# Large loads in two halves of 64 partitions, one issued by SyncE and one by ScalarE: a decode block on one core of a Trainium2 chip

## The chip, the cores and the metric

The kernel runs on one core of one Trainium2 chip. A core has TensorE (PE in the profile; its weight loads, PEld, are listed apart), VectorE (DVE), ScalarE (ACT), GpSimd (POOL), SyncE (SP), which here only issues transfers, and 16 DMA engines that move data between the chip's memory (HBM) and the on-chip memory of 128 partitions (SBUF). Each engine works through its own instructions in order; a DMA is issued by an instruction in the queue of one of the engines. The metric is the time of one execution in microseconds on the device. Most executions of one kernel agree within 0.3%.

## The reference

One decode step of a transformer block with adaptive layer norm, four sequences, one new token each, all in float32. Cut to what matters:

```python
B, Sq, D = 4, 1, 512;  H, Sk, Dh = 32, 4096, 128;  F = 1792
mod = silu(c) @ w_mod                          # six vectors of 512: sa, ca, ga, sb, cb, gb
h = layernorm(x) * (1 + ca) + sa
q = (h @ wq) as (B, H, 1, Dh)
scores = einsum("bhqd,bhkd->bhqk", q, k_cache) * Dh ** -0.5
o = einsum("bhqk,bhkd->bhqd", softmax(scores), v_cache)
x = x + ga * (o @ wo)
h = layernorm(x) * (1 + cb) + sb
out = x + gb * (silu(h @ w1) @ w2)
```

The two caches are 4 x 32 x 4096 x 128 float32 each, 268 MB apiece. Every byte of them is read once and used for one multiplication and one addition.

## The kernel before

**Tiles.** A cache tile holds four heads of one sequence: 4 heads x 4096 positions are spread over 128 partitions, 128 positions to a partition, so that a partition receives one contiguous run of 128 x 128 float32 (64 KB) and a tile has 8 MB. There are N = 32 such tiles of K and 32 of V, n = 0 to 31, with b = n % 4 the sequence and t = n // 4 the group of heads.

**Three slots.** All large data live in three slots of 64 KB per partition (`Slot`, pool `kv`, `bufs=3`), which are taken in turn: w_mod, wq, k0, v0, k1, v1, ... So k(n+1) takes the slot of v(n-1), and v(n+1) that of k(n). A load is issued when the last reader of what its slot held has finished. The first slot, that of w_mod, also holds the small tensors of the opening (`cg`, `csT`, `qs`, `zsel`), and v0 takes it.

**Order.** The body stands under `manual_schedule()`: each engine issues its instructions in the order in which the program emits them. Before the change all large loads go through `fetch` (L84) or stand at L126 and L129, on SP's queue. ACT issues four small loads of `c` at the start (L123), four of `x` in iteration 28, and two of the four output writes.

**Opening.** `c` lands, silu and a transpose make `csT` (L174, L175, L178); `mods` multiplies it with w_mod (L190, L202); after the layer norm come q = h @ wq (L237), its spreading over partitions (L247, L252) and the first four rows of q (`make_qb(0)`: four Copies on ACT at L260, a matmul at L262, one Copy at L266). Then v0 can be loaded.

**Iteration n** emits, in this order: `load_k(n+1)`; the product K x q in place, 40 of the 128 positions on POOL and 88 on DVE (`mult`, L271); `make_qb(n+1)` (ACT L266; where n+1 is a multiple of four also ACT L260 and PE L262 ahead of it); `vsum(n-1)`, two matmuls on PE at L324 that are the last readers of v(n-1); the sums over Dh on DVE (`red`, L276); the row maximum and its spreading (`rowmax` L280, `bmax` L284 on PE, `negmax` L289 to L292); the exponential on ACT and its layout on POOL (`softexp`, L298, L302); `load_v(n+1)`; the first 32 positions of V multiplied and added on POOL (`vmult`, L314, L318); and the other 96 on PE (`pv`, L339).

**End.** The last K tile is loaded in two cuts along the free dimension; wo is loaded in iteration 31 in four cuts into the slot of the last V but one, w1 and w2 in nine cuts behind the last softmax, all by `fetch`. Then follow the projection, the second layer norm and the feed-forward part.

Of the kernel before, what the change touches and what calls it, by code (L numbers as in the profile page):

```python
# [17 lines left out]
def kernel(  # L18
# [13 lines left out]
    nc = tc.nc  # L32
    P = 128
# [8 lines left out]
    NJ = HP * S // P  # L42
# [13 lines left out]
    N = B * NT  # L56
# [11 lines left out]
    class Slot:  # L68
# [4 lines left out]
        def take(self, *shape):  # L73
# [5 lines left out]
            names = " ".join(f"a{i}" for i in range(len(shape)))  # L79
            return v.rearrange(f"p ({names}) -> p {names}", **{f"a{i}": s for i, s in enumerate(shape)})  # L80

    def fetch(t, src, *cuts):
        for lo, hi in zip(cuts, cuts[1:]):
            nc.sync.dma_start(t[:, lo:hi], src[:, lo:hi])  # L84
# [3 lines left out]
    def load(dst, cache, name, n, *cuts):  # L88
        t, b = divmod(n, B)
        dst[n] = Slot(f"{name}{n}").take(NJ, Dh)  # L90
        src = cache[b, HP * t : HP * (t + 1)].rearrange("h (p j) d -> (h p) j d", p=QW)
        fetch(dst[n], src, *(cuts or (0, NJ)))

    def load_k(n, *cuts):
        load(kt, kc, "k", n, *cuts)

    def load_v(n):
        load(vt, vc, "v", n)

    wmv = wm.rearrange("(p k) n -> p k n", p=P)  # L100
    wqv = wq.rearrange("(p k) n -> p k n", p=P)
# [5 lines left out]
    wmt = s0.take(NK, 6 * D)  # L107
# [15 lines left out]
        nc.scalar.dma_start(cg[W * g : W * g + B, :], c[:, g * P : (g + 1) * P])  # L123
    for g in range(G):
        nc.gpsimd.dma_start(x0[W * g : W * g + B, :], xr[:, g * P : (g + 1) * P])
    nc.sync.dma_start(wmt, wmv)  # L126
    s1 = Slot("wq")
    wqt = s1.take(NK, H * Dh)
    nc.sync.dma_start(wqt, wqv)  # L129
    load_k(0)  # L130

    ident = const.tile([P, P], F32, name="ident")
# [123 lines left out]
    def make_qb(n):  # L256
        if n % B == 0:
            m = work.tile([P, B, Dh], F32, tag="o", name=f"qm{n}", bufs=1)
            for b in range(B):
                nc.scalar.activation(m[:, b, :], qn, AF.Copy, scale=sel[:, n + b : n + b + 1])  # L260
            p = psum([P, B, Dh], "q", 2)
            nc.tensor.matmul(p, blk.rearrange("p i x -> p (i x)"), m, start=True, stop=True)  # L262
            for b in range(B):
                qb[n + b] = p[:, b, :]
        qw[n] = work.tile([P, Dh], F32, tag="qw", name=f"qw{n}")
        nc.scalar.activation(qw[n], qb[n], AF.Copy)  # L266
# [3 lines left out]
    def mult(eng, src, n, lo, hi):  # L270
        eng.tensor_mul(  # L271
            kt[n][:, lo:hi, :], kt[n][:, lo:hi, :], src[n].unsqueeze(1).to_broadcast([P, hi - lo, Dh])
        )

    def red(n, lo, hi):
        nc.vector.tensor_reduce(sc[n][:, lo:hi], kt[n][:, lo:hi, :], axis=AX.X, op=ALU.add)  # L276

    def rowmax(n):
        nm[n] = work.tile([P, 1], F32, tag="rm", name=f"rm{n}")
        nc.vector.tensor_reduce(nm[n], sc[n], axis=AX.X, op=ALU.max)  # L280

    def bmax(n):
        p = psum([P, P], "mx", 2)
        nc.tensor.transpose(p, nm[n].to_broadcast([P, P]), ident)  # L284
        nm[n] = p

    def negmax(n):
        m = work.tile([P, HP], F32, tag="hx", name=f"hx{n}")
        nc.vector.tensor_reduce(m, nm[n].rearrange("p (i x) -> p i x", i=HP), axis=AX.X, op=ALU.max)  # L289
        nc.vector.tensor_mul(m, m, hn)  # L290
        nm[n] = work.tile([P, 1], F32, tag="nm", name=f"nm{n}")
        nc.vector.tensor_reduce(nm[n], m, axis=AX.X, op=ALU.add)  # L292

    def softexp(n):
        t, b = divmod(n, B)
        if b == 0:
            rs[t] = work.tile([P, B], F32, tag="rs", name=f"rs{t}")
        nc.scalar.activation(sc[n], sc[n], AF.Exp, bias=nm[n], accum_out=rs[t][:, b : b + 1])  # L298
        for h in range(2):
            f = first(n) if h == 0 else 0  # L300
            m = HG - f
            nc.gpsimd.tensor_mul(  # L302
                pz[h][:, f * W : HG * W].rearrange("p (g x) -> p g x", g=m)[:, :, E:].rearrange("p g (i j) -> p g i j", i=HP),
                sc[n][:, JJ * (HG * h + f) : HG * JJ * (h + 1)].rearrange("p (g j) -> p g j", j=JJ)
                .unsqueeze(2).to_broadcast([P, m, HP, JJ]),
                hm.unsqueeze(1).unsqueeze(3).to_broadcast([P, m, HP, JJ]),
            )

    def first(n):
        return NV // JJ if n < N - 2 else 0  # L310

    def vmult(n):
        if first(n):
            nc.gpsimd.tensor_mul(  # L314
                vt[n][:, :NV, :], vt[n][:, :NV, :], sc[n][:, :NV].unsqueeze(2).to_broadcast([P, NV, Dh])
            )
            for m in (NV // 2, NV // 4, JJ):
                nc.gpsimd.tensor_add(vt[n][:, :m, :], vt[n][:, :m, :], vt[n][:, m : 2 * m, :])  # L318

    def vsum(n):  # L320
        t, b = divmod(n, B)
        q, a = divmod(b, 2)
        o = (1 - a) * E
        nc.tensor.matmul(  # L324
            po[t, q][0:W, :], hs[:, o : o + W], vt[n][:, :JJ, :].rearrange("p j d -> p (j d)"),
            start=False, stop=a == 1,
        )
# [20 lines left out]
    def gather(t, q):  # L348
        o = work.tile([P, JJ, Dh], F32, tag="o", name="o", bufs=1)
        nc.vector.tensor_mul(  # L350
            o, po[t, q].rearrange("p (j d) -> p j d", j=JJ), jm.unsqueeze(2).to_broadcast([P, JJ, Dh])
        )
        if q == 0:
            od[t] = psum([P, Dh], "od", 1)
        s = work.tile([P, Dh], F32, tag="lnu", name="s", bufs=1)
        nc.vector.tensor_reduce(s, o.rearrange("p j d -> p d j"), axis=AX.X, op=ALU.add)  # L356
        nc.tensor.matmul(od[t], spick[:, 2 - 2 * q : 2 - 2 * q + P], s, start=q == 0, stop=q == 1)  # L357
# [3 lines left out]
    def norm(t):  # L361
        p = psum([P, B], "mx", 2)
        nc.tensor.matmul(p, blk.rearrange("p i x -> p (i x)"), rs[t], start=True, stop=True)
        m = work.tile([P, B], F32, tag="dx", name="dx")
        nc.vector.tensor_mul(m, p, xm)
        rd[t] = work.tile([P, 2], F32, tag="rd", name="rd")
        nc.vector.tensor_reduce(rd[t][:, 0:1], m, axis=AX.X, op=ALU.add)
        nc.vector.reciprocal(rd[t][:, 1:2], rd[t][:, 0:1])

    def spread(t):  # L370
        on = work.tile([P, R, QW], F32, tag="lnu", name="on", bufs=1)
        nc.vector.tensor_scalar(
            on, od[t].rearrange("p (x r) -> p r x", r=R), rd[t][:, 1:2], None, op0=ALU.mult
        )
        ot = work.tile([P, R, W], F32, tag="ot", name="ot", bufs=1)
        nc.vector.transpose(ot, on)
        nc.vector.tensor_copy(oz[:, t], ot[:, :, :B])
# [14 lines left out]
    for n in range(N):  # L392
        t, b = divmod(n, B)
        if n < N - 2:
            load_k(n + 1)
        elif n == N - 2:
            load_k(n + 1, 0, NJ // 2, NJ)
        else:
            so = Slot("wo")
            wot = so.take(NT, R, D)  # L400
            fetch(wot, wov, 0, NT // 2, NT - 2, NT - 1, NT)
        if n == N - B:
            for g in range(G):
                nc.scalar.dma_start(xg[W * g : W * g + B, :], xr[:, g * P : (g + 1) * P])
        sc[n] = work.tile([P, NJ], F32, tag="sc", name=f"sc{n}")
        if n + 1 < N:
            mult(nc.gpsimd, qw, n, 0, NA)
            mult(nc.vector, qb, n, NA, NJ)
            make_qb(n + 1)
            if n and first(n - 1):  # L410
                vsum(n - 1)
            red(n, NA, NJ)
        else:
            for lo in (0, NJ // 2):
                mid, hi = lo + NL // 2, lo + NJ // 2
                mult(nc.gpsimd, qw, n, lo, mid)
                mult(nc.vector, qb, n, mid, hi)
                red(n, mid, hi)
        if n and b == 0:
            gather(t - 1, 1)  # L420
        if b == 2:
            gather(t, 0)
        if n + 1 < N:
            red(n, 0, NA)
        else:
            for lo in (0, NJ // 2):
                red(n, lo, lo + NL // 2)
        if n and b == 0:
            spread(t - 1)
        rowmax(n)  # L430
        bmax(n)
        negmax(n)
        softexp(n)
        if n + 1 < N:
            load_v(n + 1)
        else:
            s2 = Slot("w12")
            w1t = s2.take(NK, F)
            w2t = s2.take(NI, D)
            fetch(w1t, w1v, 0, 2, 3, 4)  # L440
            fetch(w2t, w2v, 0, 4, 8, 11, 12, 13, 14)
        if b == B - 1:
            norm(t)
        vmult(n)
        pv(n)
# [74 lines left out]
```

## Time and profile before

| what | value |
|---|---|
| time, median of 3 runs | 1323.12 us (1322.90 to 1323.14) |
| the profiled execution's own time | 1323.02 us |
| its span, first to last instruction | 1321.1 us |
| moved by DMA | 567.66 MB, 430 GB/s over the span |
| busy: DVE | 1011.0 us (77%) |
| busy: POOL | 844.9 us (64%) |
| busy: PE | 381.0 us (29%) |
| busy: ACT | 45.2 us (3%) |

The share of an engine is the time in which it worked on instructions, over the span; registers, branches, waits and the issuing of DMAs are not counted. A DMA queue has a row of its own: q1 carries what SP issues, q10 what ACT issues, q0 what POOL issues; q8 and q14 load instructions. Its packets, bytes and the share of the 16 DMA engines' time that they took stand beside it. In a timeline line stand the start, the duration, the engine, the line of the program and the operation; in brackets the idle time before it and what ended that.

### The profile page before, as it was taken

The numbers are of one execution on the slowest core, as the hardware profiler recorded it, in microseconds if no ns is written. First come the engines' busy times: TensorE is split into PE (matmuls) and PEld (weight loads), VectorE is DVE, ScalarE is ACT, GpSimd is POOL, SyncE is SP. The second block draws the span as 40 slices with busy tenths as digits, with TensorE's granted clock in tenths as the row PEclk, the third lists the DMA queues.
The fourth block names the chain that finished last, engine by engine and source line by source line (L and its number), as shares of the span: only waits on it lengthen the run. The fifth ranks groups of instructions, "written<-read, shape, count | busy, mean of one in ns | idle before, by whom it ended". The sixth has DMA issues, their size and how long they took to land.

```text
span 1321.1 us, 5438 instructions
## 1 busy us (share of the span) xinstructions
PE 381.0 (29%) x2114; PEld 98.8 (7%) x2114; DVE 1011.0 (77%) x362; ACT 45.2 (3%) x148; POOL 844.9 (64%) x231
## 2 busy tenths in 40 slices
PE   3421133222222233222322322233321223322047
PEld 0100000000000000000000000000000000000013
DVE  2378877877888777898778788787779877787982
ACT  1100000000000000000000000000000000000001
POOL 1236787575678756577865756877565786657550
PEclk9855666665566666566666556666655666655569
DMA  9999999999999999999999999999999999999998
GB/s 413 443 415 442 439 421 437 437 427 437 433 431 435 435 431 433 433 435 433 433 427 437 435 429 435 439 429 429 439 429 433 441 429 429 434 437 429 425 425 341
DMA packets 12282, 567.66 MB, mean 430 GB/s; under 512 B 1441, under 2 KB 1505, under 8 KB 2273
## 3 DMA queue, kind: packets, MB, share of 16 engines
q1 hardware_dynamic: 12048, 567.29, 99.5%
q8 instruction: 17, 0.28, 0.1%
q14 instruction: 9, 0.07, 0.0%
q0 software_dynamic: 128, 0.01, 0.0%
q10 hardware_dynamic: 80, 0.02, 0.0%
HBM read 567.30 MB, written 0.01 MB: 429 GB/s over the span
## 4 chain that ended last, share of the span: by engine, by line
DVE 39%; DMA 32%; POOL 19%; another core or an unknown queue 4%; PE 3%; issue 2%; ACT 1%; DVEq 0%; POOLq 0%; ACTq 0%
DMA k<-in_A_k_cache_dram 29%; DVE sc L276 21%; DVE k L271 14%; POOL v L318 9%; POOL v L314 8%; DMA w<-in_B_w_dram 3%; PE po L324 2%; DVE s L356 1%; POOL pz L302 1%; POOL k L271 1%; DVE o L350 1%; ACT sc L298 1%; PE mx L284 1%; DVE hx L289 0%
## 5 line engine op out<-in xcount | busy, mean ns | idle before, releaser
L276 DVE TENSOR_REDUCE sc<-k 128x88 f32<-128x11264 f32 (+2 forms) x66 | 554.4, 8422 | 1.1
L271 DVE TENSOR_TENSOR k<-k,q 128x11264 f32<-128x11264 f32 (+1 forms) x33 | 378.4, 11467 | 217.9 <-DMA k<-in_A_k_cache_dram 217.9
L271 POOL TENSOR_TENSOR k<-k,qw 128x5120 f32<-128x5120 f32 (+1 forms) x33 | 356.2, 10796 | 53.1 <-DMA k<-in_A_k_cache_dram 53.1
L302 POOL TENSOR_TENSOR pz<-sc,hm 128x128 f32<-128x128 f32 (+1 forms) x64 | 31.5, 512 | 378.7 <-ACT sc L298 378.7
L339 PE MATMUL po<-v,pz 128*32 128x512 f32 x1568 | 239.5, 775 | 44.3 <-POOL pz L302 44.2
L318 POOL TENSOR_TENSOR v<-v 128x2048 f32<-128x2048 f32 (+2 forms) x90 | 244.6, 2717 | 7.1
L314 POOL TENSOR_TENSOR v<-v,sc 128x4096 f32<-128x4096 f32 x30 | 211.0, 7033 | 0.0
L324 PE MATMUL po<-v,hs 128*32 128x512 f32 x60 | 57.4, 1061 | 249.4 <-POOL v L318 249.4
L284 PE MATMUL mx<-ident,rm 128*128 128x128 f32 x32 | 14.5, 454 | 385.9 <-DVE rm L280 385.9
L357 PE MATMUL od<-s,spick 128*128 128x128 f32 x32 | 12.2, 484 | 217.5 <-DVE s L356 217.5
L339 PEld LDWEIGHTS po<-v,pz 128*32 128x32 f32 x1568 | 56.3, 138 | 205.7 <-issue 154.1
L284 PEld LDWEIGHTS mx<-ident,rm 128*128 128x128 f32 x32 | 5.8, 182 | 417.4 <-issue 272.3
L298 ACT ACTIVATE sc<-sc,nm 128x128 f32<-128x128 f32 x32 | 12.8, 401 | 694.8 <-DVE nm L292 694.8
L266 ACT ACTIVATE qw<-q 128x128 f32<-128x128 f32 x32 | 8.9, 277 | 505.1 <-DVE k L271 446.7
L324 PEld LDWEIGHTS po<-v,hs 128*32 128x32 f32 x60 | 5.4, 140 | 276.1 <-POOL v L318 276.1
L357 PEld LDWEIGHTS od<-s,spick 128*128 128x128 f32 x32 | 7.8, 303 | 244.2 <-DVE s L356 129.3
L289 DVE TENSOR_REDUCE hx<-mx 128x4 f32<-128x128 f32 x32 | 9.3, 292 | 19.7 <-PE mx L284 19.7
L350 DVE TENSOR_TENSOR o<-po,jm 128x512 f32<-128x512 f32 x16 | 10.9, 682 | 9.1 <-PE po L339 9.1
L356 DVE TENSOR_REDUCE s<-o 128x128 f32<-128x512 f32 x16 | 16.3, 1020 | 0.6
L190 PE MATMUL q<-wm 128*32 128x512 f32 x48 | 10.0, 723 | 20.5 <-DVE wm L178 20.5
L198 DVE TENSOR_TENSOR wm<-q,hm 64x256 f32<-64x256 f32 (+1 forms) x8 | 4.1, 549 | 9.2 <-PE q L190 8.3
L260 ACT ACTIVATE qm<-qn,sel 128x128 f32<-128x128 f32 x32 | 10.1, 387 | 0.0
(95 smaller groups left out, 137.6 us busy)
## 6 DMA issues: line engine op xcount, KB each, us to landing
k<-in_A_k_cache_dram SPq DMA_DIRECT2D x2, 4096.0 KB
wm<-in_w_mod_dram SPq DMA_DIRECT2D x1, 6144.0 KB
wo<-in_A_wo_dram SPq DMA_DIRECT2D x1, 4096.0 KB
wo<-in_A_wo_dram SPq DMA_DIRECT2D x1, 2048.0 KB
wo<-in_A_wo_dram SPq DMA_DIRECT2D x2, 1024.0 KB, 33.0
w<-in_B_w_dram SPq DMA_DIRECT2D x2, 1024.0 KB
w<-in_B_w_dram SPq DMA_DIRECT2D x1, 1792.0 KB
w<-in_B_w_dram SPq DMA_DIRECT2D x2, 896.0 KB
```

What stands on the lines that cost most here:

```text
L271: eng.tensor_mul(kt[n][:, lo:hi, :], kt[n][:, lo:hi, :], src[n].unsqueeze(1).to_broadcast([P, hi - lo, Dh]))
L276: nc.vector.tensor_reduce(sc[n][:, lo:hi], kt[n][:, lo:hi, :], axis=AX.X, op=ALU.add)
L284: nc.tensor.transpose(p, nm[n].to_broadcast([P, P]), ident)
L298: nc.scalar.activation(sc[n], sc[n], AF.Exp, bias=nm[n], accum_out=rs[t][:, b : b + 1])
L302: nc.gpsimd.tensor_mul(pz[h][:, f * W : HG * W].rearrange("p (g x) -> p g x", g=m)[:, :, E:].rearrange("p g (i j) -> p g i j", i=HP), sc[n ...
L314: nc.gpsimd.tensor_mul(vt[n][:, :NV, :], vt[n][:, :NV, :], sc[n][:, :NV].unsqueeze(2).to_broadcast([P, NV, Dh]))
L318: nc.gpsimd.tensor_add(vt[n][:, :m, :], vt[n][:, :m, :], vt[n][:, m : 2 * m, :])
L324: nc.tensor.matmul(po[t, q][0:W, :], hs[:, o : o + W], vt[n][:, :JJ, :].rearrange("p j d -> p (j d)"), start=False, stop=a == 1,)
L339: nc.tensor.matmul(po[t, q][W * g : W * (g + 1), :], pz[h][:, o : o + W], vt[n][:, JJ * j : JJ * (j + 1), :].rearrange("p j d -> p (j d)") ...
L350: nc.vector.tensor_mul(o, po[t, q].rearrange("p (j d) -> p j d", j=JJ), jm.unsqueeze(2).to_broadcast([P, JJ, Dh]))
L356: nc.vector.tensor_reduce(s, o.rearrange("p j d -> p d j"), axis=AX.X, op=ALU.add)
L357: nc.tensor.matmul(od[t], spick[:, 2 - 2 * q : 2 - 2 * q + P], s, start=q == 0, stop=q == 1)
```

## The change

A new helper `both` issues a load as two DMAs: partitions 0 to 63 from SP, partitions 64 to 127 from ACT. `load` (all K and V tiles, the cuts of the last K tile included) and the loads of w_mod and wq use it. wo, w1 and w2 stay with `fetch` on SP. In the loop `load_v(n + 1)` is emitted ahead of `softexp(n)` and no longer behind it, so that on ACT the issue stands ahead of the exponential; in the last iteration, which loads w1 and w2 instead, the order stays as it was.

```diff
+    def both(t, src):
+        nc.sync.dma_start(t[: P // 2], src[: P // 2])
+        nc.scalar.dma_start(t[P // 2 :], src[P // 2 :])
+
     def fetch(t, src, *cuts):
...
         src = cache[b, HP * t : HP * (t + 1)].rearrange("h (p j) d -> (h p) j d", p=QW)
-        fetch(dst[n], src, *(cuts or (0, NJ)))
+        cuts = cuts or (0, NJ)
+        for lo, hi in zip(cuts, cuts[1:]):
+            both(dst[n][:, lo:hi], src[:, lo:hi])
...
-    nc.sync.dma_start(wmt, wmv)
+    both(wmt, wmv)
     s1 = Slot("wq")
     wqt = s1.take(NK, H * Dh)
-    nc.sync.dma_start(wqt, wqv)
+    both(wqt, wqv)
     load_k(0)
...
         negmax(n)
-        softexp(n)
         if n + 1 < N:
             load_v(n + 1)
-        else:
+        softexp(n)
+        if n + 1 == N:
             s2 = Slot("w12")
```

## The prediction, made before the result was known

> **What bounds the kernel now.** I read the page's head and its table of DMA queues first, then busy time by stage, then the chain of work that ended last.
>
> ```profile
> span 1321.1 us, 5438 instructions
> DMA packets 12282, 567.66 MB, mean 430 GB/s; under 512 B 1441, under 2 KB 1505, under 8 KB 2273
> q1 hardware_dynamic: 12048, 567.29, 99.5%
> ...
> DVE 39%; DMA 32%; POOL 19%; another core or an unknown queue 4%; PE 3%; issue 2%; ACT 1%; DVEq 0%; POOLq 0%; ACTq 0%
> ```
>
> SP's queue alone, q1, keeps all 16 DMA engines at work for 99.5% of the span: 0.995 x 1321.1 = 1314.5 us. Only 6.6 us are left that a better supply could win, 0.5% of the time. The chain shows DVE at 39%, but it follows semaphores, and a transfer that lies behind another one in the DMA engines looks to it like waiting for the engine that released it. By stage:
>
> ```profile
> core 0: us, PE busy (x) PEld busy (x) DVE busy (x) ACT busy (x) POOL busy (x), PEclk, DMA share, GB/s
> 0.00:18.00 18.00, 0.00 (x0) 0.00 (x0) 3.21 (x21) 0.00 (x0) 4.24 (x14) 1.00 0.99 409
> 18.00:58.00 40.00, 25.95 (x150) 8.23 (x150) 7.22 (x19) 7.39 (x18) 0.00 (x0) 0.94 0.97 420
> 58.00:1280.00 1222.00, 324.22 (x1653) 78.21 (x1653) 990.21 (x295) 33.41 (x122) 839.52 (x215) 0.59 1.00 433
> 1280.00:1321.00 41.00, 30.83 (x311) 12.37 (x311) 10.34 (x28) 4.45 (x8) 1.18 (x2) 0.83 0.87 358
> ```
>
> From 58 to 1280 us the DMA share is 1.00 at 433 GB/s, 27.06 GB/s per DMA engine, so a row of 64 KB (one partition of a cache tile) takes 65,536 B / 27.06 = 2.42 us. Within an iteration the issues run well ahead of the data:
>
> ```profile
> 107.98 0.33 SPq L84 DMA_DIRECT2D k<-in_A_k_cache_dram  x1
> 126.13 0.33 SPq L84 DMA_DIRECT2D v<-in_A_v_cache_dram  x1
> 127.70 0.40 ACT L298 ACTIVATE sc<-sc,nm 128x128 f32<-128x128 f32 x1 [18.54 <-DVE nm L292]
> 135.82 11.89 DVE L271 TENSOR_TENSOR k<-k,q 128x11264 f32<-128x11264 f32 x1 [8.15 <-DMA k<-in_A_k_cache_dram]
> ```
>
> When the V load was issued at 126.13, the K load ahead of it still had 135.8 - 126.1 = 9.7 us to go. That is the cover for anything that delays an issue. The time is set by bytes over rate, and the question is what the change does to the rate.
>
> **The change, part by part.**
>
> *Issuing.* 31 of the 32 K loads and all V loads become two instructions, the last K load four, and w_mod and wq four together; ACT receives 32 + 33 + 2 = 67 new ones. The nearest row for one is this:
>
> ```profile
> 1.04 1.87 ACTq L123 DMA_DIRECT2D wm<-in_c_dram  x4
> ```
>
> 1.87 / 4 = 0.47 us each, 31 us in all on an engine that is busy for 45.2 of 1321 us: not a bound. Where it waits, who is behind it? ACT's half of v(n+1) waits for the same DVE end as SP's (126.13) and would be issued by 126.6; L298 behind it could not start before 127.70 anyway. ACT's half of k(n+1) waits for L324; behind it stands L266:
>
> ```profile
> 106.04 1.92 PE L324 MATMUL po<-v,hs 128*32 128x512 f32 x2 [8.47 <-POOL v L318]
> 108.88 0.28 ACT L266 ACTIVATE qw<-q 128x128 f32<-128x128 f32 x1 [19.34 <-DVE k L271]
> ```
>
> L266 starts at 108.88, after the 107.98 + 0.47 at which the issue would be over. Both cost nothing; without that cover they would cost up to 0.47 us an iteration, against the 9.7 us just named. Moving `load_v` ahead of `softexp` likewise only spares the upper half the 1.6 us from 126.13 to 127.70 and the exponential, which the 9.7 us hide in any case.
>
> *How two queues share a DMA engine.* The opening shows it, because there ACT's four small loads of c run beside SP's rows. These are the DMA queues' rows for 4.2 to 6.0 us, then for 13.4 to 15.2 us, then who waited for c:
>
> ```profile
> q1 hardware_dynamic: 16, 0.79, 102.9%
> q10 hardware_dynamic: 4, 0.00, 0.4%
> ...
> q1 hardware_dynamic: 16, 0.79, 100.9%
> ...
> q10 hardware_dynamic: 4, 0.00, 0.1%
> ...
> 18.10 1.28 ACT L174 ACT_TABLE_LOAD   x1 [18.10 <-DMA wm<-in_c_dram]
> ```
>
> In each stretch, one row of SP per engine (16), and on four of the engines one tiny packet of ACT. Eight stretches like these pass until c is there, at 18.10, though its bytes are nothing. So an engine takes whole rows by turns from the two queues; it does not run them side by side. After the change every engine will write one row of the lower half, then one of the upper half, and so on.
>
> *The rate of a half.* Here is the unknown. In the trace every large row goes at 27.06 GB/s per engine, from weights and caches alike, so the limit isn't the source; it sits in the engine or in the 8 partitions that are its share of a 128-partition load. If in the engine, the change costs nothing here: 1314.5 us of rows stay 1314.5. If in the partitions, a half offers 64 / 8 = 8 such shares, 216.5 GB/s, and all depends on whether the engines write the same half at the same time. Rows start nearly together; these are the bytes by time in the first 18 us, in slices of 0.45 us, each row counted where it starts:
>
> ```profile
> GB/s 0 0 0 546 1092 109 0 0 0 1096 656 0 0 659 1093 0 0 547 1205 0 0 547 1205 0 0 438 1314 0 0 328 1315 109 0 328 1206 218 0 291 1607 437
> ```
>
> All 16 starts fall into two or three slices and then nothing for two or three. Two engines are thus apart by a few tenths of a microsecond, at most about 0.9, of a row of 2.42 us, and nothing in equal turns moves them apart. Not split are wo, w1 and w2:
>
> ```profile
> wo<-in_A_wo_dram SPq DMA_DIRECT2D x1, 4096.0 KB
> wo<-in_A_wo_dram SPq DMA_DIRECT2D x1, 2048.0 KB
> wo<-in_A_wo_dram SPq DMA_DIRECT2D x2, 1024.0 KB, 33.0
> w<-in_B_w_dram SPq DMA_DIRECT2D x2, 1024.0 KB
> w<-in_B_w_dram SPq DMA_DIRECT2D x1, 1792.0 KB
> w<-in_B_w_dram SPq DMA_DIRECT2D x2, 896.0 KB
> w<-in_B_w_dram SPq DMA_DIRECT2D x1, 768.0 KB
> w<-in_B_w_dram SPq DMA_DIRECT2D x3, 256.0 KB, 17.8
> ```
>
> These are 15,360 KB, 15.7 MB. Split are 567.3 - 15.7 = 551.6 MB, 1273.8 us at 433 GB/s. So the ends for this term are 0 and +1273.8 us. I take the upper one, lessened by the start spread: as a load has landed only with its last row, the engines that are least apart decide, and I put the doubled share at 0.95 (an offset of 0.12 us in 2.42), an estimate between 1 and the 1 - 0.9 / 2.42 = 0.63 of the widest spread: +1210 us. Why the upper end: one and the same speed for rows of all kinds fits either place, but only the partitions change in this edit, and the turns put all engines on one half.
>
> [...]
>
> *The opening.* c's packets now stand in ACT's queue ahead of the upper half of w_mod. On the four engines that carry them, that half starts only at 18.1 us, and each of its 4 rows (48 KB, 1.81 us) then takes turns with a row of wq or k0 (2.42 us): 18.1 + 4 x 4.23 = 35.0 us at an unchanged rate, where L190 needed it at 20.52.
>
> ```profile
> 20.52 6.41 PE L190 MATMUL q<-wm 128*32 128x512 f32 x16 [20.52 <-DVE wm L178]
> 45.79 0.33 SPq L84 DMA_DIRECT2D v<-in_A_v_cache_dram  x1
> 58.18 11.89 DVE L271 TENSOR_TENSOR k<-k,q 128x11264 f32<-128x11264 f32 x1 [20.05 <-DMA k<-in_A_k_cache_dram]
> ```
>
> So v0 would be issued at 45.8 + 14.5 = 60.3 and its rows start about 1 us later, while the queues run empty at about 57, when k0 ends: +4 us (0 to 7). With doubled rows this vanishes: the three first loads then last until about 110, and even with w_mod at 70 us v0 is issued at 95.
>
> **Sum.** 1323.0 + 1210 + 0 (opening) + 0 (issuing) = 2533 us. The profiled time is 0.1 us under the median, which changes nothing.
>
> **Rivals.**
>
> *The limit is the engine's, and the opening costs its gap:* 1323 + 4 = 1327 us (1326 to 1330). For it: equal rates for rows of every size. Against it: no row shows fewer than 128 partitions loaded fast.
>
> *The engines fall out of step.* If one engine of two that share partitions gets a little more of them, it runs ahead until it writes the upper half while the other writes the lower, and the loss shrinks; half out of step gives 1323 + 637 = 1960 us. Against it: turns of equal rows keep an offset as it is.
>
> *Not slower.* The rate holds, and w_mod lands before 20.5 + 11.2 = 31.7 us, since k0's end (57) less the first microsecond and the 45.8 of v0's issue leaves about that much cover: then no gap arises, and the time is 1323. For more than a tie some of the 6.6 us would have to be won, most of which lies at the end, in loads that stay as they are.
>
> *The change does not do what it says.* ACT's half of k4 waits for L324 of tile 2. Take the rows around it:
>
> ```profile
> 168.80 1.26 ACT L260 ACTIVATE qm<-qn,sel 128x128 f32<-128x128 f32 x4
> 176.42 1.12 PE L262 MATMUL q<-qm,blk 128*128 128x512 f32 x2
> 185.38 1.92 PE L324 MATMUL po<-v,hs 128*32 128x512 f32 x2 [7.83 <-POOL v L318]
> 187.32 0.33 SPq L84 DMA_DIRECT2D k<-in_A_k_cache_dram  x1
> ```
>
> L324 stands behind L262 on PE, L262 needs L260 from ACT, and in emission order L260 stands behind that very issue: a ring of waits. So in these iterations (n = 3, 7, ..., 27) ACT must issue its half elsewhere, behind L260 or L266. It is released by the same L324, so the price is nothing; were the halves kept on one queue, the time would be 1323.
>
> **Chances.** In step (own range 2390 to 2600): 0.50. Partly out of step: 0.14. Rate kept with a gap at the opening: 0.24. Not slower: 0.12, of which 0.03 is faster; a measurement here tells about 0.2%, 2.6 us, from no change. That gives slower 0.88, same 0.09, faster 0.03. The range has to reach from the second case to the first: 1325 to 2600.
>
> **What would show it.** Right: DMA share still near 1.00 but GB/s near 220 in the middle stages, rows of 64 KB that take nearly 5 us, q1 and q10 with about equal bytes, DVE waiting for K most of the time. Rival one: 433 GB/s in the middle, and a stretch without data near 57 to 61 us with L190 starting near 35. Partly out of step: a rate between, which changes along the run. The prediction is wrong if the middle runs at 433 GB/s.

## The result, and the profile after

| | before | after |
|---|---|---|
| time, median | 1323.11 us (1322.90 to 1323.22, 6 runs) | 2594.43 us (2579.83 to 2607.39, 6 runs) |
| ratio to before | | 1.960, 95% interval 1.954 to 1.967 |
| the profiled execution's own time, span | 1323.02 us, 1321.1 us | 2595.29 us, 2593.5 us |

The change makes the kernel twice as slow. These are lines of the page of the changed kernel: its span, the DMA engines over 40 slices, the queues, the chain, and the costliest wait of DVE. Lines behind L81 have moved: `mult` is now L277, `red` L282, `vsum` L330.

```profile
span 2593.5 us, 5593 instructions
...
DMA  9999999999999999999999999999999999999998
GB/s 211 210 210 211 210 210 213 218 215 212 212 218 217 212 223 216 224 226 239 246 211 215 219 212 211 213 221 212 210 214 218 214 214 219 215 218 212 215 244 294
...
q1 hardware_dynamic: 7760, 291.51, 50.7%
q10 hardware_dynamic: 5440, 275.80, 49.1%
...
another core or an unknown queue 44%; DVE 34%; DMA 16%; issue 3%; POOL 2%; PE 1%; DVEq 0%; POOLq 0%
...
L277 DVE TENSOR_TENSOR k<-k,q 128x11264 f32<-128x11264 f32 (+1 forms) x33 | 378.4, 11467 | 1400.8 <-DMA k<-in_A_k_cache_dram 1400.8
```

The DMA engines are as busy as before and move the same bytes, but at 219 GB/s on the mean; the two queues share them half and half. DVE does the same 378.4 us of products and now waits 1400.8 us for K, where it waited 217.9. This is the same line of the page before:

```profile
L271 DVE TENSOR_TENSOR k<-k,q 128x11264 f32<-128x11264 f32 (+1 forms) x33 | 378.4, 11467 | 217.9 <-DMA k<-in_A_k_cache_dram 217.9
```

The stages of the changed kernel, in the columns of the stage table before:

```profile
core 0: us, PE busy (x) PEld busy (x) DVE busy (x) ACT busy (x) POOL busy (x), PEclk, DMA share, GB/s
0.00:60.00 60.00, 0.00 (x0) 0.00 (x0) 3.91 (x23) 1.59 (x2) 4.26 (x14) 1.00 1.00 210
60.00:130.00 70.00, 26.63 (x150) 8.52 (x150) 16.04 (x18) 5.80 (x16) 9.47 (x1) 0.81 1.01 210
130.00:2500.00 2370.00, 324.31 (x1621) 84.26 (x1625) 954.53 (x289) 34.13 (x122) 816.59 (x213) 0.55 1.00 217
2500.00:2593.00 93.00, 35.27 (x351) 13.37 (x343) 36.55 (x33) 4.45 (x8) 16.72 (x4) 0.70 0.93 281
```

A DMA share of 1.00 from the start to 2500 us says that no stretch was lost by a late issue. The whole loss is in the rate. In the trace's records of single packets a row of 64 KB takes 4.89 us (median of 8192), against 2.42 before; rows of w1, which are not split, take 0.275 us as before (7 KB, median).

How the rows lie in time shows the step. These are the queues' rows in three stretches of the changed kernel: 136.5 to 139.5 us, 141.5 to 144.5 us, and 1240 to 1245 us (packets counted where they start):

```profile
q1 hardware_dynamic: 16, 1.05, 164.1%
...
q10 hardware_dynamic: 16, 1.05, 165.2%
...
q1 hardware_dynamic: 14, 0.92, 74.7%
q10 hardware_dynamic: 3, 0.20, 16.0%
```

In the first stretch 16 rows of the lower half start, as many as there are engines, and none of the upper; 5 us later 16 of the upper half start. (The share is over 100% because the rows run past the end of the stretch.) At 1240 us the two are mixed, and there the rate is a little higher:

```profile
140.00:200.00 60.00, 10.12 (x51) 2.40 (x51) 10.60 (x7) 1.78 (x3) 16.11 (x6) 0.56 1.00 210
1200.00:1290.00 90.00, 8.85 (x51) 2.70 (x51) 48.52 (x11) 0.77 (x3) 38.16 (x8) 0.54 1.01 246
```

Over the whole run this picture holds less and less. The packet records give, at any time, how many of the sixteen rows under way belong to the lower half and how many to the upper. All sixteen are on one half for 55% of the time from 140 to 700 us, for 30% from 700 to 1500 us and for 14% from 1500 to 2450 us, while the rate is 213, 221 and 215 GB/s. By stretches of 20 us the rate does rise with the mixing, but little: 210 GB/s where on the mean less than one engine is on the other half (6 stretches), 216 with two to three (67 stretches), 239 with four to six (7 stretches). If each half took 216 GB/s from whichever engines write to it, five engines on one half and eleven on the other would give 5 x 27.06 + 216 = 351 GB/s, by estimate. So the loss does not need all engines on one half, and mixing them is not enough to end it.

The theory put to the test, P, as it stood when the experiments were planned: a half of 64 partitions takes only half the rate while all engines write to it, and whole rows keep the engines on the same half. The main rival, Q: two queues that take turns on an engine are what costs.

### The profile page after: what moved, and what is told of

It reads as the page before. It is cut to its first block, busy times and chain, and to the rows that moved or that the text cites. A ratio compares the mean times of both kernels' runs of the same rounds, so it can differ in the third digit from the quotient of the medians.

```text
span 2593.5 us, 5593 instructions
## 1 busy us (share of the span) xinstructions
PE 386.2 (15%) x2114; PEld 106.2 (4%) x2114; DVE 1011.0 (39%) x362; ACT 46.0 (2%) x148; POOL 847.0 (33%) x231
## 4 chain that ended last, share of the span: by engine, by line
another core or an unknown queue 44%; DVE 34%; DMA 16%; issue 3%; POOL 2%; PE 1%; DVEq 0%; POOLq 0%
DVE sc L282 19%; DMA k<-in_A_k_cache_dram 14%; DVE k L277 13%; DMA w<-in_B_w_dram 2%; POOL k L277 1%; POOL v L324 1%; POOL v L320 1%; DVE s L362 1%; PE mx L290 0%; PE q L196 0%; DVE o L356 0%; DVE hx L295 0%; DVE rm L286 0%; DVE hx L296 0%
## 5 line engine op out<-in xcount | busy, mean ns | idle before, releaser
L277 DVE TENSOR_TENSOR k<-k,q 128x11264 f32<-128x11264 f32 (+1 forms) x33 | 378.4, 11467 | 1400.8 <-DMA k<-in_A_k_cache_dram 1400.8
L277 POOL TENSOR_TENSOR k<-k,qw 128x5120 f32<-128x5120 f32 (+1 forms) x33 | 357.4, 10832 | 824.4 <-DMA k<-in_A_k_cache_dram 814.3
L282 DVE TENSOR_REDUCE sc<-k 128x88 f32<-128x11264 f32 (+2 forms) x66 | 554.4, 8422 | 1.1
L330 PE MATMUL po<-v,hs 128*32 128x512 f32 x60 | 57.5, 1061 | 187.9 <-POOL v L324 187.9
L268 PE MATMUL q<-qm,blk 128*128 128x512 f32 x16 | 15.6, 1078 | 437.6 <-ACT qm L266 437.6
L345 PEld LDWEIGHTS po<-v,pz 128*32 128x32 f32 x1568 | 62.7, 137 | 374.2 <-issue 359.4
L196 PE MATMUL q<-wm 128*32 128x512 f32 x48 | 9.4, 690 | 68.7 <-DMA wm<-in_w_mod_dram 68.7
L266 ACT ACTIVATE qm<-qn,sel 128x128 f32<-128x128 f32 x32 | 10.2, 389 | 514.7 <-DVE rm L286 514.7
```

The source lines that it names most:

```text
L277: eng.tensor_mul(kt[n][:, lo:hi, :], kt[n][:, lo:hi, :], src[n].unsqueeze(1).to_broadcast([P, hi - lo, Dh]))
L330: nc.tensor.matmul(po[t, q][0:W, :], hs[:, o : o + W], vt[n][:, :JJ, :].rearrange("p j d -> p (j d)"), start=False, stop=a == 1,)
L345: nc.tensor.matmul(po[t, q][W * g : W * (g + 1), :], pz[h][:, o : o + W], vt[n][:, JJ * j : JJ * (j + 1), :].rearrange("p j d -> p (j d)") ...
```

## The experiments

**Two queues, halves along the row.** Both queues, the number of DMAs and their order stay; each half goes to all 128 partitions.

```diff
     def both(t, src):
-        nc.sync.dma_start(t[: P // 2], src[: P // 2])
-        nc.scalar.dma_start(t[P // 2 :], src[P // 2 :])
+        h = t.shape[1] // 2
+        nc.sync.dma_start(t[:, :h], src[:, :h])
+        nc.scalar.dma_start(t[:, h:], src[:, h:])
```

> The halves are cut along the row instead of across the partitions: SP brings the first half of each partition's run, ACT the second, both to all 128 partitions; queues, number of DMAs, and order are those of the change. Theory P (64 partitions take only half the rate, and all engines write the same half at a time): the middle runs at about 433 GB/s again, a row of 32 KB takes 1.21 us. The ring of waits around k4, k8, ... k28 stays, so these loads are issued behind the sums of their iteration, some 16 us later than before (203.6 instead of 187.3 there), against about 6 us of cover: +10 us seven times, and about +4 us at the opening: 1323 + 74 = 1397 us (1330 to 1410). Rival Q (two queues that take turns on an engine are what costs): as the change, 2590 us, 215 GB/s.

Measured: 1425.87 us, 1.078 times before (1.075 to 1.080), above the expected 1330 to 1410. Rows of 32 KB take 1.216 us: full rate. Q falls. Most of what is left, 103 us, is idle time of the DMA engines: by their packets 97 us, against 5 before. This is the table by stage around the first gap:

```profile
170.00:194.00 24.00, 7.72 (x49) 1.89 (x49) 16.86 (x6) 0.50 (x2) 21.68 (x7) 0.64 0.93 399
194.00:208.00 14.00, 0.00 (x0) 0.00 (x0) 13.30 (x3) 0.54 (x2) 5.37 (x1) 0.50 0.00 0
208.00:366.00 158.00, 44.45 (x212) 10.62 (x212) 113.60 (x36) 3.83 (x15) 105.41 (x28) 0.59 0.99 425
```

From 194 to 208 us nothing is moved. There are seven such gaps of 11 to 14 us, 82 us together, one in each iteration n = 3, 7, ... 27. The changed kernel shows what happens there; this is its timeline in iteration 3:

```profile
382.66 5.47 DVE L282 TENSOR_REDUCE sc<-k 128x40 f32<-128x5120 f32 x1
388.16 0.47 SPq L83 DMA_DIRECT2D k<-in_A_k_cache_dram  x1
388.16 0.50 ACTq L84 DMA_DIRECT2D k<-in_A_k_cache_dram  x1
...
388.71 1.28 ACT L266 ACTIVATE qm<-qn,sel 128x128 f32<-128x128 f32 x4 [76.12 <-DVE rm L286]
390.04 2.08 PE L268 MATMUL q<-qm,blk 128*128 128x512 f32 x2 [64.00 <-ACT qm L266]
392.04 1.92 PE L330 MATMUL po<-v,hs 128*32 128x512 f32 x2
...
393.99 0.47 SPq L83 DMA_DIRECT2D v<-in_A_v_cache_dram  x1
```

ACT did keep its emission order: k4 is issued at 388.16, ahead of the Copies at L266. It could, because k4 no longer waits for `vsum` at L330 (392.04 to 393.96). It starts when the last sum of K ends (382.66 + 5.47 = 388.13), which frees the slot of k3; v4 then follows the end of L330, which frees that of v2. The two loads have exchanged slots, and k4 is issued a stage later.

**The same, with ACT's half of K emitted later.** `load` keeps ACT's half of a K load back, and the loop emits it behind `vsum(n - 1)`.

```diff
                 vsum(n - 1)
+            flush()
             red(n, NA, NJ)
```

> As the run before it, and ACT's half of each K load is emitted behind the two matmuls that free its slot, so that no ring of waits arises. P: 433 GB/s throughout, only the opening's gap is left: 1327 us (1323 to 1331). The difference to the run before is the price of the ring at full rate, 74 us by estimate. Q: 2590 us.

Measured: 1329.66 us, 1.0047 times before (1.0030 to 1.0064). The gaps are gone:

```profile
core 0: us, PE busy (x) PEld busy (x) DVE busy (x) ACT busy (x) POOL busy (x), PEclk, DMA share, GB/s
0.00:58.00 58.00, 29.57 (x150) 8.78 (x150) 10.43 (x40) 7.12 (x17) 4.26 (x14) 0.94 0.98 415
58.00:1280.00 1222.00, 326.33 (x1654) 78.87 (x1653) 982.59 (x293) 33.70 (x123) 839.81 (x215) 0.59 1.00 431
```

The exchange of slots costs 1425.9 - 1329.7 = 96 us at full rate. The rest, 6.5 us, is not a gap at the opening (DMA share 0.98 to 58 us, in which before had 0.97 to 0.99): the middle runs at 431 GB/s instead of 433, 0.5% of 1222 us, about 5.7 us.

**Halves of 64 partitions, one queue.** `nc.scalar` becomes `nc.sync` in `both`.

> Halves of 64 partitions as in the change, but both issued by SP, so that only one queue carries large loads. P: an engine writes its lower rows, then its upper ones, and all engines are still on the same half: rows of 64 KB take 4.84 us, 2590 us (2500 to 2600). Q: 1323 us.

Measured: 2705.53 us, 2.045 times before (2.041 to 2.049), above the expected 2500 to 2600. The loss needs no second queue; it needs the halves. Rows take 5.13 us (median), which is 6% more than twice 2.42.

**Another half.** SP brings partitions 32 to 95, ACT the rest in two DMAs.

```diff
-        nc.sync.dma_start(t[: P // 2], src[: P // 2])
-        nc.scalar.dma_start(t[P // 2 :], src[P // 2 :])
+        nc.sync.dma_start(t[32:96], src[32:96])
+        nc.scalar.dma_start(t[:32], src[:32])
+        nc.scalar.dma_start(t[96:], src[96:])
```

> SP brings partitions 32 to 95, ACT 0 to 31 and 96 to 127. If any 64 partitions take only half the rate: both queues' rows at 4.84 us, 2590 us. [...] Q: 2590 us, both queues' rows alike.

Measured: 2758.60 us, 2.085 times before (2.081 to 2.089). That is more than the 2590 expected if any 64 partitions take half the rate, and that case is not what happened. At the very start SP's rows are alone on the engines. These are the DMA rows of this kernel from 4.6 to 6.5 us, when 16 rows of 48 KB of partitions 32 to 95 start:

```profile
DMA packets 16, 0.79 MB, mean 414 GB/s; under 512 B 0, under 2 KB 0, under 8 KB 0
...
q1 hardware_dynamic: 16, 0.79, 95.5%
```

And these are the 16 rows of partitions 0 to 63 at the same place of the changed kernel, from 5.1 to 9.0 us:

```profile
DMA packets 20, 0.79 MB, mean 202 GB/s; under 512 B 0, under 2 KB 4, under 8 KB 4
...
q1 hardware_dynamic: 16, 0.79, 99.0%
```

Each row takes 1.82 us in the first and 3.85 in the second. So it is not any 64 partitions that are slow: 0 to 63 are, 32 to 95 are not. In both runs a row goes to a single partition, and in the kernel before rows to all partitions take 2.42 us for 64 KB, so by these times the limit is not within one engine's row; engines hinder each other by which partitions they write at the same time. Once ACT's rows of 32 partitions run between them, SP's rows lose this: their median over the run is 4.62 us, from 2.42 up to 8.

**The three parts from one queue.** All three DMAs of the run before go to SP, one behind the other.

> SP issues all three parts of each load: partitions 32 to 95, then 0 to 31, then 96 to 127, one behind the other, so that engines do not mix them. If 32 to 95 are conflict-free among themselves and the others are shared by two engines each: half the rows at 2.42 us, half at 4.9 to 5.13, (4 x 2.42 + 4 x 5.0) / (8 x 2.42) = 1.53 times the time of the split bytes: 1323 + 0.53 x 1274 = 2000 us (1900 to 2100). If any 64 partitions are slow, and the run with the middle half was slow for that: 2700 us.

Measured: 2596.63 us, 1.962 times before (1.958 to 1.966). The expectation of 1.53 times as long is 433 / 1.53 = 283 GB/s; by stage the run has:

```profile
0.00:60.00 60.00, 16.99 (x76) 4.51 (x80) 10.44 (x40) 4.37 (x10) 4.25 (x14) 0.91 0.99 280
60.00:300.00 240.00, 43.02 (x235) 12.25 (x227) 91.81 (x23) 8.07 (x23) 81.34 (x21) 0.56 1.01 257
300.00:700.00 400.00, 53.94 (x265) 14.22 (x265) 155.15 (x48) 4.79 (x18) 135.65 (x35) 0.54 1.00 216
700.00:2500.00 1800.00, 244.64 (x1231) 64.68 (x1231) 717.13 (x218) 23.58 (x89) 608.99 (x157) 0.54 1.00 213
```

It begins at 280 GB/s, is down to 216 behind 300 us and to 213 behind 700, so neither number of the expectation came out. At the start the middle part did run at full rate: 47 of the 128 rows of 48 KB took 1.82 us, and 27% of the rows of 64 KB that start before 300 us take under 2.6 us. Behind 300 us only 0.5% do. That rows of different parts then run at the same time and hinder each other is likely, but one queue carries them all and the trace does not tell them apart; why this ends as slow as the pure lower half was not shown.

**Only the opening in halves.** `both` for w_mod and wq, all K and V loads whole.

> Only w_mod and wq are given in halves; all K and V loads are whole again, on SP. Theory P: 14.7 MB at half rate cost 14.7 MB / 0.433 = 34 us more, c lands at 34 us, w_mod near 67, v0 is issued near 103 as in the change, while the rows of k0 end near 92: about 11 us more: 1368 us (1350 to 1385). If only a lasting state of the loop is slow: 1323 to 1331 us.

Measured: 1392.51 us, 1.052 times before (1.050 to 1.054), +69 us instead of +45. This is its timeline:

```profile
34.09 1.28 ACT L178 ACT_TABLE_LOAD   x1 [34.09 <-DMA wm<-in_c_dram]
70.65 6.21 PE L194 MATMUL q<-wm 128*32 128x512 f32 x16 [70.65 <-DMA wm<-in_w_mod_dram]
...
114.98 9.67 PE L241 MATMUL q<-wq,wm 128*32 128x512 f32 x64 [26.42 <-DMA wq<-in_A_wq_dram]
...
124.71 0.35 SPq L88 DMA_DIRECT2D v<-in_A_v_cache_dram  x1
```

wq is complete only at 115 us and v0 is issued at 124.7; from 114.5 to 125.7 us the DMA engines stand still. The 23.07 MB of w_mod, wq and k0 are there only at 114.5 us; before, k0 ended at about 57. They went at 210 GB/s up to 70 us and at 207 from 70 to 95 us, so the whole rows of k0 that took turns with upper rows of wq gained nothing, and at 161 from 95 to 115 us, where the DMA share is only 0.73. That makes 57 + 11 us.

**The change, with ACT's half of K emitted later.** The edit of the second experiment, on the halves of the change.

> The change, with ACT's half of each K load emitted behind the two matmuls that free its slot: no ring of waits, the loads take their slots in the old order. Rows of the two halves still run in step at about 4.88 us and 20 us or more of rows are queued at each late issue of the change, so theory P expects no gain from it: 2590 us (2560 to 2610). If the ring costs as much here as at full rate (97 us there): 2500 us.

Measured: 2528.95 and 2636.51 us, on either side of the change's 2594.43 (2579.83 to 2607.39) and too far apart for a verdict: whether late emission gains anything at half rate is not decided, and 2500 is not excluded. That the exchange of slots costs nothing in the change itself rests on its DMA share of 1.00. In the faster execution, the profiled one, the rate drifts, from 213 GB/s (130 to 900 us) over 224 (900 to 1700) to 239 (1700 to 2400).

**Setting half of the engines apart.** Three runs on the kernel of the run before. GpSimd, a third queue, issues a copy within the chip's memory in iteration 2, which was meant to hold up 8 of the 16 engines.

```diff
+            if n == 2:
+                nc.gpsimd.dma_start(scr, kc[0, 0].rearrange("(p j) d -> p (j d)", p=32)[:8])
```

> As the run before it, and in iteration 2 GpSimd issues one copy of 8 rows of 64 KB within the chip's memory, which is 0.5 MB more to move. If the loss is that the two engines that share partitions write the same half at the same time, and if these 8 rows go to 8 neighbouring engines, engine 0 to 7, this sets them one row behind engines 8 to 15 and one half is written by the one while the other writes the other: the middle goes to rows of 2.42 us and 433 GB/s after it, about 1323 + 6 + 130 (the doubled rows until 260 us) = 1460 us (1400 to 1700 with a part of the engines still in step). If the step has nothing to do with it (each engine pays for 64 partitions by itself), or the rows go to other engines: as the run before it, 2590 us.

Measured: 2577.69 and 2627.16 us. The copy went out as 16 packets of 32 KB between 297.8 and 307.3 us, and not as 8 rows of 64 KB; that each packet fell to another engine, as the next expectation takes it, no record shows. The next two runs cut it to rows with gaps; the second of them issues only the first of the three copies.

```diff
+                rows = kc[0, 0].rearrange("(p j) d -> p (j d)", p=32)
+                for i, w in enumerate((7168, 128, 7168)):
+                    nc.gpsimd.dma_start(scr[8 * i : 8 * (i + 1), :w], rows[8 * i : 8 * (i + 1), :w])
```

> In e6_out_of_step the copy had become 16 packets of 32 KB, one on each engine, so that no engine was set apart from another; nothing was tested. Here GpSimd issues in iteration 2 a copy of 8 rows of 28 KB, one of 8 rows of 512 B, and another of 8 rows of 28 KB, with gaps between the rows so that each stays 8 packets. If the first and the third meet the same 8 engines, these are 2 x 1.2 us behind the other 8, one row of 2.42 us, and of two engines that share partitions one writes the lower half while the other writes the upper: rows go to 2.42 us, 433 GB/s from about 300 us on, 1323 + 6 + 148 = 1480 us (1450 to 1700). If the step has nothing to do with the loss: 2590 us.

> Only the first of the three copies: 8 engines are half a row behind the other 8. If the step is the cause, engines that share partitions meet for half of each row: 1.5 times 2.42 us per row on the mean, 290 GB/s from 300 us on: about 2040 us (1900 to 2200). If not: 2590 us.

Measured: 2640.77 us (1.996 times before, 1.992 to 2.000) and 2621.63 us (1.981, 1.977 to 1.985). The packets were as meant, 8 of 28 KB for each long copy. The stages of the first of the two, ahead of the copies (at 297 to 337 us) and behind them:

```profile
130.00:290.00 160.00, 19.97 (x102) 4.70 (x102) 61.08 (x15) 2.83 (x7) 55.23 (x15) 0.54 1.00 210
350.00:450.00 100.00, 9.73 (x53) 2.72 (x53) 41.46 (x11) 0.49 (x2) 38.01 (x8) 0.53 1.00 211
```

Nothing changed in the rate. But the copies did not bring half of the engines onto the other half, either. In both runs every round behind them, up to 390 us, is still sixteen rows of one half; their starts lie within 2.0 to 3.2 us of each other, against 2.1 to 2.7 us in the rounds before the copies, while a row takes 4.9 us (packet records). Rows that start behind a copy are shorter, down to 4.55 us. So against the expectation both runs are misses, and they are no test of P, since the state for which it expects a gain did not arise. The trace does not say which engine carried a packet, so it stays open whether the engines that hinder each other were held up alike, whether a copy that writes no partition delays an engine whose row waits for partitions, or whether the engines fell back into step. The step itself stays unproven.

**Short rows.** The same halves from the same two queues, ACT's half of K late as before, but every half of a K or V load becomes two DMAs, each with every second 2 KB of a partition's run, so that a row is 2 KB. w_mod and wq keep their long rows.

```diff
+            cut = [v[:, lo:hi].rearrange("p (a b c) d -> p b a (c d)", b=2, c=4) for v in (dst[n], src)]
+            for u in range(2):
+                d, s = cut[0][:, u], cut[1][:, u]
+                first_half(d, s)
+                late.append((d, s))
```

> As e5_halves_late_k, with each K and V load cut so that a row is 2 KB instead of 64 KB: every half becomes two DMAs that take every second 2 KB of a partition's run. An engine then changes between lower and upper half every 2 KB. If the loss comes from whole rows, during which all engines stay on one half, and an engine has more than one row of 2 KB under way, both halves are written at the same time and the loss goes: rows of 2 KB go at 24.1 GB/s where loads are whole (84 to 85 ns, the last loads of w2), so 1323 + 1274 x (27.06 / 24.1 - 1) = 1480 us (1400 to 1700). If changing sooner doesn't help (what an engine has under way is one row, or the engines change together at any length): 2590 us or more, up to 2 x 1.12 x 1274 + 50 = 2900 us.

Measured: 1611.59 us, 1.218 times before (1.202 to 1.234), against 2528.95 and 2636.51 with long rows. By stage:

```profile
0.00:60.00 60.00, 0.00 (x0) 0.00 (x0) 3.37 (x22) 1.59 (x2) 4.24 (x14) 1.00 1.00 211
60.00:120.00 60.00, 25.90 (x150) 8.22 (x150) 29.84 (x21) 6.08 (x17) 11.03 (x1) 0.78 1.00 332
120.00:1500.00 1380.00, 321.02 (x1584) 98.45 (x1584) 923.25 (x281) 32.61 (x119) 800.39 (x209) 0.57 1.04 362
```

One run holds both: 211 GB/s while the long rows of w_mod and wq go (the last of them ends at 73.6 us), 362 GB/s in halves of 64 partitions when the rows are short. Unsplit loads of 2 KB rows have 2048 B / 85 ns x 16 = 386 GB/s (the last loads of w2), so the halves keep 94% of what rows of this length give. The division between the halves shows in the rate: in stretches of 1 us between 120 and 1500 us it is 365 GB/s where each half gets at least 45% of the rows (1322 stretches), and 237 where one gets over three quarters (6 stretches). The loss is therefore not in halves as such: it goes with the long rows and, within this run, with the stretches in which one half gets most of the rows. The expected 1480 us were too low, by 123 in the profiled execution (1602.75): the slow opening was left out of the sum (14.7 MB of w_mod and wq at 211 instead of 386 GB/s, 32 us), and the loads of K and V have 362 instead of 386 GB/s (537 MB, 92 us).

**The other part of the change alone.** The load of V ahead of the exponential, all loads whole on SP.

> Only the other part of the change: the load of V is emitted ahead of the exponential, all loads whole and on SP. SP's own order stays as it was, so nothing moves: 1323 us, within 0.2%, by every theory.

Measured: 1323.17 us, 0.9999 times before (0.9989 to 1.0008). It is nothing by itself.

## Why the prediction was right, and where it was not

- **What bounds the kernel:** right. DMA bytes over DMA rate set the time before and after (567.7 MB at 430 and at 219 GB/s), and DVE's 39% of the chain were no bound.
- **Issuing:** right. ACT's issues of K and V take 0.50 us in the median (0.47 estimated) and delay nothing (DMA share 1.00); the order of `load_v` and `softexp` moves nothing (0.9999).
- **Whole rows by turns, all engines on one half:** right near the start, as the 16 rows of q1 and the 16 of q10 in the two stretches near 140 us show. "Nothing in equal turns moves them apart" is wrong: the time with all engines on one half falls from 55% to 14% along the run, and the loss stays. That long rows are what costs was shown by the short rows. That two engines share partitions and lose when both are on the same half, as a rival of the prediction and the expectations of the runs with copies take it, was the author's assumption and was not shown: no record says which engines hinder each other, and the copies did not set them apart.
- **The rate of a half:** right in its value (210 GB/s against 216.5), and right to put the limit into the partitions and not into the engine. It was wrong in its generality. "A half offers 64 / 8 = 8 such shares" does not hold for every half: partitions 32 to 95 alone took 1.82 us for a row for which 0 to 63 took 3.85.
- **The share of 0.95:** wrong in size. The loss is 2595.3 - 1323.0 = 1272.3 us, 0.999 of the 1273.8. The start spread did not save the 5% that the estimate gave it. In the run with one queue the rows took 6% over a doubling (5.13 us), and stretches like that at 1240 us, 246 GB/s, give some of it back; that the two come out so near a plain doubling is luck. 2533 was 62 us, 2.4%, below the profiled execution.
- **The range:** 1325 to 2600 covers nearly every case that was considered, so that the result lies in it says little. The first case's own range, 2390 to 2600, holds the median with 6 us to spare; one of the six executions, 2607.39, lies above it.
- **The opening:** right that it costs no gap in the change: the DMA share is 1.00 and 1.01 up to 130 us. w_mod was there at 68.7 us (70 in the prediction), v0 issued by SP at 102.6 (95).
- **The rival with the rate kept, 1327 us:** the kernel with halves along the row gives 1329.7, the right size for another reason, a rate 0.5% lower. Its "equal rates for rows of every size" holds in the kernel before for rows of 32 to 64 KB (26.9 to 27.1 GB/s per engine) and not for those of 2 KB (24.1). The gap itself was not tried with halves of partitions at full rate.
- **The rival "Not slower":** 57 less 1 less 45.8 leaves 10.2 us of cover, not 11.2; its time does not change by it.
- **The ring of waits:** the ring was seen, and its price was wrong. "ACT must issue its half elsewhere" did not happen: ACT kept its order and the loads exchanged slots. "The price is nothing" holds only under the slow rows; with the rate kept it is 96 us. So the rival that kept the rate would have ended near 1425, not at 1327, with the edit as it was.

## What to carry to other kernels

Before dividing a load between queues, look at the DMA share. Here it was 1.00 in the loop, a second queue had nothing to give, and what changed the rate was the length of the rows and the partitions that they write to. Cutting the load along the row, with all 128 partitions in each DMA, kept 431 of 433 GB/s here; where it was cut into halves of 64 partitions, long rows were the worse case (217 GB/s with 64 KB, 362 with 2 KB). And where an engine that computes also issues loads, follow its waits through every engine: a load that would have waited for work behind its own instruction got another slot here, and came late, which cost 96 us where the rate was full.

## What the runs showed of the hardware that was not expected

- Two halves of the same size behave differently: 48 KB rows to partitions 32 to 95 took 1.82 us while they were alone, to 0 to 63 3.85 us.
- Mixing does not mend it: with on the mean four to six of the sixteen engines on the other half, the rate was 239 GB/s, with less than one 210.
- Halves cost more than twice 2.42 us for a row of 64 KB: 5.13 us instead of 4.84 when one queue brings half after half (2705 us), 4.89 when two queues take turns (2594 us; both medians).
- The executions of the changed kernel spread over 1% (2579.83 to 2607.39), those of it with ACT's half of K emitted later over 4% (2528.95 to 2636.51), where the six of the kernel before lie within 0.03% (1322.90 to 1323.22).
